# Decoding float64 weights in one two-slope ScalarE pass, and padding the first query block's attention weights to 128 rows

## The chip, the cores and the metric

The kernel runs on one core of a Trainium2 chip. The metric is the device time of one launch in microseconds (us), lower is better. Before the change the median of three runs is 1122.09 us (1118.11 to 1125.32).

The engines, as the profile names them: PE is TensorE's matrix multiply and PEld its weight load, DVE is VectorE, ACT is ScalarE, POOL is GpSimd, and SP is SyncE, which in this kernel issues every DMA. Each engine works through its own queue in order.

## The reference, cut to what matters

```python
def _attn_ref(q, k, v, f):                 # q, k, v: (8, 8, 576, 64), f: (8, 8, 576)
    scores = scale * np.matmul(q, k.transpose(0, 1, 3, 2))
    cum = np.cumsum(np.log(np.clip(f, 0.0001, 1.0)), axis=-1)
    decay = cum[:, :, :, None] - cum[:, :, None, :]
    scores = np.where(causal, -1000000000.0, scores + decay)
    attn = np.exp(scores - np.max(scores, axis=-1, keepdims=True))
    attn = attn / (np.sum(attn, axis=-1, keepdims=True) + 1e-09)
    return np.matmul(attn, v)

def _moe_ref(x, w_in, w_out):              # x: (4608, 512), w_in: (512, 2048), w_out: (2048, 512)
    h = x @ w_in
    g = h * np.clip(h + 3.0, 0.0, 6.0) / 6.0
    return (g @ w_out)
```

Eight batches of eight heads go through causal attention with a decay, and the result, 4608 tokens of 512 features, through two matrix products with a hard-swish between them. `w_in` and `w_out` are float64, 8 MB each; the kernel gets them as 64-bit integers and has to make fp16 of them.

## The kernel before, in words

**Attention.** The list `VH` has 68 units. Four "A" units take two heads of batch 0 each, queries 0 to 255; eight "B" units take one head of batch 0 each, queries 256 to 575; 56 "F" units take one head of batches 1 to 7 each, all 576 queries. An F unit is `rows(v)`. It cuts the queries into five chunks that start at `RB` and have `RR = [64, 128, 128, 128, 128]` rows, so chunk 0 has 64 queries and the others 128. The chunks are done in two halves, `NAT = ((1, 4, 0), (2, 3))`. For a half, PE makes the scores `pn` (lines 623 and 626), DVE masks them and takes the row maximum into `pp` (L634), ACT takes the exponential (L646) and rounds it to fp16 (L658), and DVE or POOL subtract to get the low fp16 part (L661, L667, L672). High and low part lie side by side in `hl`, one of three buffers `ring` that the weight decoding used earlier. Then `dma_start_transpose` (L685) turns blocks of 128 columns of `hl` into `pT`, so that keys lie on partitions. There is one such DMA for neighbouring chunks with equal rows: in the first half one for chunks 1 and 4 (12 blocks of 128 rows) and one for chunk 0 (one block of 64 rows), in the second half one for chunks 2 and 3 (12 blocks).

`av(v, ph)` multiplies `pT` with the values: for each chunk `c` the weights of PE are a block of `pT` (128 keys by the chunk's queries), and the moving operand is the values' 65 columns (64 and a column of ones) or their low part. Lines 713 and 714 are the first two products of each chunk, lines 716 to 718 the rest. For chunk 0 there are only those two, and their weights are 64 columns wide.

**Weights.** `w_in` and `w_out` come in 16 chunks each of 128 by 512 float64 values (512 KB). `w_load` issues the DMA into a slot, `w_decode` makes float32 of it, and a Square with an accumulator (L271) sums the squares for a power-of-two scale; the slot is free for the next load when that Square, which writes its unused output there, is done. `w_split` later makes the fp16 high and low parts. In `w_decode` the high 32-bit word of the double, read as a float32 and scaled by 2^-112, has its exponent where a shift by three bits makes a float32 of it, with the top three bits of the low word behind it. The tables `POOL_SIGN` choose between two ways of keeping the sign. For 15 of the 32 chunks two ACT Relu passes (L254, L255) make the two signs' parts, POOL adds them (L256), and DVE shifts the low word (L257) and joins (L258). For the other 17 one ACT Copy (L262) is followed by three DVE operations: shift the low word (L263), put the sign bit into it (L264), join (L267).

**The rest.** Nine tiles of 512 tokens go through `h_unit` (lines 800 to 802 on PE, then L810, L813, L814, L815 on ACT and DVE) and `out_unit` (lines 822 to 824, then L833). The first tile needs the decoded `w_in`, and its second part the split `w_out`.

**What sets the order.** The text of the main loop interleaves the attention units with steps of the weight work (`w_step`, by `W_RATE`) and with steps of the token tiles (`fill`, by `F_RATE`). From that text a scheduler with a timing model of its own lays out each engine's queue: it places an instruction where its model finds the inputs ready. So a change in one place can move instructions of other places in every queue. On PE the products of the token tiles stand between those of the attention.

## Time and profile before

| | us |
|---|---|
| median of three runs (lowest, highest) | 1122.09 (1118.11, 1125.32) |
| the profiled execution's own time | 1118.29 |
| its span in the trace | 1116.5 |
| PE busy | 1040.3 |
| DVE busy | 745.9 |
| ACT busy | 619.5 |
| POOL busy | 430.4 |

The granted TensorE clock was 0.977 of full speed over the span. Busy matmuls are pipelined and their ends are modelled, so a busy PE is not PE at its peak; the start of one matmul to the start of the next is the better measure of what PE spends on it. The chain of waits follows the work that ended last back from the end, and names at each step what released it.

### The profile page before, as it was taken

To read this page: it belongs to the slowest core of one execution; us is meant where nothing else is said; L and a number is where in the kernel's file an instruction comes from. 1 tells how busy PE (TensorE), PEld (TensorE's weight loads), DVE (VectorE), ACT (ScalarE), POOL (GpSimd) and SP (SyncE) were. 2 spreads that over 40 slices of the span, in tenths; PEclk is the share of its full clock that TensorE was granted. 3 is DMA by queue.
4 is the path that set the end of the run, shared out by engine and by line. 5 is a ranking of instruction groups with operands and counts; after the bars stand their busy time and mean duration, and the time that the engine had idled before them with its cause. 6 is when DMAs were issued, how large, how long until landed. Compare 5 with 4: busy or idle time off the path is not lost.

```text
span 1116.5 us, 20389 instructions
## 1 busy us (share of the span) xinstructions
PE 1040.3 (93%) x7074; PEld 582.4 (52%) x7074; DVE 745.9 (67%) x1921; ACT 619.5 (55%) x1300; POOL 430.4 (39%) x464
## 2 busy tenths in 40 slices
PE   1779897899899998999999989999999999999998
PEld 1457774575455554554555545554555554444443
DVE  7987998787795679668865886587658951520520
ACT  4667765656773466537754764476547841621520
POOL 8565563336444444434443534453344420000000
PEclk9969998999999999999999989999999999999999
DMA  7664545676656565656566766556676443001001
GB/s 221 210 203 145 181 119 110 144 161 140 167 114 133 132 154 109 126 129 165 116 125 131 148 127 124 130 126 136 127 129 134 95 98 60 10 1 38 1 1 38
DMA packets 259859, 132.84 MB, mean 119 GB/s; under 512 B 227652, under 2 KB 229244, under 8 KB 259756
## 3 DMA queue, kind: packets, MB, share of 16 engines
q1 hardware_dynamic: 259756, 131.54, 52.1%
q8 instruction: 56, 0.92, 0.3%
q14 instruction: 47, 0.39, 0.1%
HBM read 47.93 MB, written 9.73 MB: 52 GB/s over the span
## 4 chain that ended last, share of the span: by engine, by line
PE 66%; DVE 15%; DMA 8%; SPq 4%; issue 3%; ACT 3%; POOL 1%; DVEq 0%; ACTq 0%; POOLq 0%
PE po L823 10%; PE po L822 10%; PE po L824 10%; PE ph L800 8%; PE ph L801 8%; PE ph L802 8%; PE pn L626 3%; PE pn L623 3%; DMA ring<-in_w_out_dram 2%; DVE pp L634 2%; DVE ring L661 1%; SPq L774 1%; DMA xT<-xhl 1%; PE pav L717 1%; PE pav L718 1%
## 5 line engine op out<-in xcount | busy, mean ns | idle before, releaser
L800 PE MATMUL ph<-xT,w 128*128 128x512 f16 (+1 forms) x640 | 232.2, 364 | 20.2 <-DVE r L813 15.3
L801 PE MATMUL ph<-xT,w 128*128 128x512 f16 (+1 forms) x640 | 231.0, 364 | 0.0
L802 PE MATMUL ph<-xT,w 128*128 128x512 f16 (+1 forms) x640 | 230.5, 363 | 0.0
L823 PE MATMUL po<-w,gT 128*128 128x512 f16 x576 | 216.6, 382 | 5.7 <-DVE w L309 5.6
L646 ACT ACTIVATE pp<-pp,nb 128x192 f32<-128x192 f32 x280 | 138.3, 552 | 142.6 <-DVE nb L640 141.9
L824 PE MATMUL po<-w,gT 128*128 128x512 f16 x576 | 216.2, 381 | 0.0
L822 PE MATMUL po<-w,gT 128*128 128x512 f16 x576 | 213.9, 382 | 0.8 <-ACT o L833 0.8
L661 DVE TENSOR_TENSOR ring<-pp,ring 128x128 f16<-128x128 f32 (+2 forms) x216 | 134.3, 638 | 86.0 <-ACT ring L658 83.5
L473 POOL TENSOR_TENSOR T<-ST,T 64x576 fp32r<-64x576 f32 (+1 forms) x68 | 102.7, 1511 | 215.7 <-DMA T<-TK 196.0
L813 DVE SCALAR_TENSOR_TENSOR r<-r,ph 128x512 f32<-128x512 f32 (+1 forms) x160 | 100.0, 626 | 89.2 <-ACT r L810 89.1
L810 ACT ACTIVATE r<-ph,bias_r,SC 128x256 f32<-128x256 f32 (+7 forms) x272 | 144.5, 571 | 23.8 <-PE ph L802 21.0
L814 ACT CAST gT<-r 128x512 f16<-128x512 f32 (+1 forms) x160 | 91.7, 575 | 83.5 <-DVE r L813 83.3
L634 DVE CUSTOM_DVE_ANT_0 pp<-pn,W 128x192 f32<-128x192 f32 x280 | 122.8, 481 | 21.3 <-PE pn L626 20.3
L815 DVE TENSOR_TENSOR gT<-r,gT 128x512 f16<-128x512 f32 (+1 forms) x160 | 115.4, 725 | 27.4 <-ACT gT L814 27.0
L623 PE MATMUL pn<-TK,TQ 68*128 68x192 f32 x336 | 125.0, 385 | 2.4 <-PE pav L724 0.9
L626 PE MATMUL pn<-T,T 128*128 128x192 f32 x336 | 113.9, 369 | 0.7 <-POOL T L473 0.7
L658 ACT CAST ring<-pp 128x192 f16<-128x192 f32 x280 | 112.6, 452 | 0.0
L461 POOL TENSOR_SCALAR TK<-ST 64x576 fp32r<-64x576 f32 (+1 forms) x68 | 57.3, 842 | 129.3 <-issue 74.6
L470 POOL TENSOR_TENSOR T<-ST,TQ 64x576 fp32r<-64x576 f32 (+2 forms) x68 | 99.6, 1464 | 16.7 <-PE pn L626 11.4
L801 PEld LDWEIGHTS <-w 128*128 128x128 f16 x640 | 62.8, 99 | 69.6 <-issue 26.1
L667 POOL TENSOR_TENSOR ring<-pp,ring 128x128 f16<-128x128 f32 x96 | 59.4, 619 | 97.3 <-ACT ring L658 81.7
L800 PEld LDWEIGHTS <-w 128*128 128x128 f16 x640 | 63.2, 99 | 62.3 <-issue 15.6
(151 smaller groups left out, 1777.7 us busy)
## 6 DMA issues: line engine op xcount, KB each, us to landing
ST<-in_qk_dram SPq DMA_DIRECT2D x64, 288.0 KB
T<-TK SPq DMA_DIRECT2D x64, 144.0 KB
out_dram<-o SPq DMA_DIRECT2D x36, 256.0 KB
ring<-in_w_out_dram SPq DMA_DIRECT2D x16, 512.0 KB
T<-TQ SPq DMA_DIRECT2D x56, 144.0 KB
vst<-in_vS_dram SPq DMA_DIRECT2D x7, 1040.0 KB
ring<-in_w_in_dram SPq DMA_DIRECT2D x9, 512.0 KB
w<-in_w_in_dram SPq DMA_DIRECT2D x7, 512.0 KB
```

Of the source, the lines that this page charges most:

```text
L623: nc.tensor.matmul(dst, TQ[i][0:D + 4, qs], TK[i][0:D + 4, a:e], start=True, stop=False)
L626: nc.tensor.matmul(dst, T7[j][:, qs], T1[j][:, a:e], start=False, stop=True)
L634: nc.vector.tensor_tensor_reduce(pp[:r, w:w + kw], pn[:r, o:o + kw], W[:r, 4 * P + r - kw:4 * P + r], 1.0, -3.0e38, ALU.add, ALU.max, accu ...
L646: nc.scalar.activation(x_, x_, AF.Exp, bias=nb[:r, e0 + x:e0 + x + 1], scale=0.125)
L661: eng.tensor_tensor(hl[:r, a:a + c * P], pp[:r, at[c] + 64:at[c] + kw], hl[:r, h0[c] + 64:h0[c] + kw], op=ALU.subtract,)
L800: nc.tensor.matmul(ph, w1[0][:, cc, fs_], xh, start=(cc == 0), stop=False)
L801: nc.tensor.matmul(ph, w1[0][:, cc, fs_], xl, start=False, stop=False)
L802: nc.tensor.matmul(ph, w1[1][:, cc, fs_], xh, start=False, stop=(cc == NCC - 1))
L810: nc.scalar.activation(r[:, a:e], ph[:, a:e], AF.Relu, bias=bias_r, scale=scol(A1 + NG * b + fc * NG // NFC))
L822: nc.tensor.matmul(po, gT[:, 0, fc, ts_], w2[:, fc, 0, :], start=(fc == 0), stop=False)
L823: nc.tensor.matmul(po, gT[:, 0, fc, ts_], w2[:, fc, 1, :], start=False, stop=False)
L824: nc.tensor.matmul(po, gT[:, 1, fc, ts_], w2[:, fc, 0, :], start=False, stop=(fc == NFC - 1))
```

## The change

It has two parts.

**The weights' decoding.** All 32 chunks go one way. ACT's Prelu with scale 2^-112 and slope 2^32 for negative inputs does what the two Relu passes and POOL's addition did: a negative number gets an exponent that is 32 higher, and one bit of that becomes the sign after the shift by three. DVE then shifts the float32 word in place, and a second DVE operation shifts the low word and joins. The slot is only read by these, where before DVE and ACT also wrote into it.

```diff
-            low = nc.gpsimd if POOL_LOW[i][k % 4] else nc.vector
-            if POOL_SIGN[i][k % len(POOL_SIGN[i])]:
-                nc.scalar.activation(f32, hf, AF.Relu, scale=2.0 ** -112)
-                nc.scalar.activation(hf, hf, AF.Relu, scale=-2.0 ** -80)
-                nc.gpsimd.tensor_tensor(f32, f32, hf, op=ALU.add)
-                low.tensor_scalar(lo, lo, 29, None, op0=ALU.logical_shift_right)
-                nc.vector.scalar_tensor_tensor(
-                    i32, i32, 3, lo, op0=ALU.logical_shift_left, op1=ALU.bitwise_or
-                )
-            else:
-                nc.scalar.activation(f32, hf, AF.Copy, scale=2.0 ** -112)
-                low.tensor_scalar(lo, lo, 29, None, op0=ALU.logical_shift_right)
-                nc.vector.scalar_tensor_tensor(
-                    lo, hi, -2 ** 31, lo, op0=ALU.bitwise_and, op1=ALU.bitwise_or
-                )
-                nc.vector.scalar_tensor_tensor(
-                    i32, i32, 3, lo, op0=ALU.logical_shift_left, op1=ALU.bitwise_or
-                )
+            nc.scalar.activation(f32, hf, AF.Prelu, scale=2.0 ** -112, alpha=2.0 ** 32)
+            nc.vector.tensor_scalar(i32, i32, 3, None, op0=ALU.logical_shift_left)
+            nc.vector.scalar_tensor_tensor(
+                i32, lo, 29, i32, op0=ALU.logical_shift_right, op1=ALU.bitwise_or
+            )
```

**The first 64 queries of an F unit.** POOL writes zeros into rows 64 to 127 of chunk 0's block of `hl`. With that all blocks of a half have 128 rows, and one transpose moves the half: 13 blocks in the first, 12 in the second. `pT` is laid out with 128 columns a block, and the products of chunk 0 have 128 rows, of which the upper 64 are zero. A single memset of the upper rows of `pav` before the first F unit goes.

```diff
-            o += (2 * c + 1) * RR[c]
+            o += (2 * c + 1) * P
...
+            if 0 in NAT[half]:
+                nc.gpsimd.memset(hl[64:, h0[0] - 64:h0[0] + 64], 0.0)
...
-            for a, e, r, d in moves:
-                g = (e - a) // P
-                nc.sync.dma_start_transpose(
-                    pT[:, d:d + g * r].rearrange("p (g t) -> p g t", t=r), hl[0:r, a:e]
-                )
+            w = sum((2 * c + 1) * P for c in NAT[half])
+            d = HT[NAT[half][0]]
+            nc.sync.dma_start_transpose(
+                pT[:, d:d + w].rearrange("p (g t) -> p g t", t=P), hl[:, 0:w]
+            )
...
-            if n == H:
-                nc.vector.memset(pav[64:, 0], 0.0)
             for c in range(NCH):
-                m = RR[c]
-                pb = ph[:, HT[c]:HT[c] + (2 * c + 1) * m].rearrange("p (g t) -> p g t", t=m)
-                o1, o0 = pav[:m, c, 0:D + 1], pav[:m, c, 0:D]
+                pb = ph[:, HT[c]:HT[c] + (2 * c + 1) * P].rearrange("p (g t) -> p g t", t=P)
+                o1, o0 = pav[:, c, 0:D + 1], pav[:, c, 0:D]
```

Three places show what that makes of the queues. The rows give the line, the operation, the tile written and the tiles read, and the size of the output; line numbers behind the decoding are 15 to 22 lower in the changed kernel.

PE, in the middle of the F units, where the values' products of one head begin. L713 and L714 are chunk 0's, the L800 group is a token tile's. Before:

```order
L801 MATMUL ph_8_0_6192<-xT_117,w_113 128x512
L713 LDWEIGHTS pT_5922
L713 MATMUL pav<-v_111,pT_5922 64x65
L802 LDWEIGHTS w_114
L802 MATMUL ph_8_0_6192<-xT_117,w_114 128x512
L800 LDWEIGHTS w_113
L800 MATMUL ph_8_0_6192<-xT_117,w_113 128x512
L714 LDWEIGHTS pT_5922
L714 MATMUL pav<-v_111,pT_5922 64x64
L801 LDWEIGHTS w_113
L801 MATMUL ph_8_0_6192<-xT_117,w_113 128x512
```

The same place in the changed kernel:

```order
L779 MATMUL ph_8_0_6144<-xT_117,w_113 128x512
L691 LDWEIGHTS pT_5874
L691 MATMUL pav<-v_111,pT_5874 128x65
L780 LDWEIGHTS w_114
L780 MATMUL ph_8_0_6144<-xT_117,w_114 128x512
L778 LDWEIGHTS w_113
L778 MATMUL ph_8_0_6144<-xT_117,w_113 128x512
L692 LDWEIGHTS pT_5874
L692 MATMUL pav<-v_111,pT_5874 128x64
L779 LDWEIGHTS w_113
L779 MATMUL ph_8_0_6144<-xT_117,w_113 128x512
```

The order here is the same; the two products of chunk 0 are 128 rows high instead of 64. In 17 of the 56 heads before, L713 and L714 of chunk 0 stand next to each other; in the other 39 a token tile's products stand between them, as here.

SP and POOL, for the same head. SP before: the head's three transposes, with a load of queries and keys (`ST`) and the loads of the next values (`vst`) behind them.

```order
L426 DMA ST_103<-in_qk_dram 128x576
L685 DMA_TRANSPOSE pT_5922<-ring_124 128x12x128
L685 DMA_TRANSPOSE pT_5922<-ring_124 128x1x64
L685 DMA_TRANSPOSE pT_5922<-ring_125 128x12x128
L426 DMA ST_104<-in_qk_dram 128x576
L374 DMA vst<-in_vS_dram 64x520 x2
L375 DMA vst<-in_vS_dram 128x4x520
```

SP in the changed kernel:

```order
L411 DMA ST_103<-in_qk_dram 128x576
L666 DMA_TRANSPOSE pT_5874<-ring_124 128x13x128
L411 DMA ST_104<-in_qk_dram 128x576
L666 DMA_TRANSPOSE pT_5874<-ring_125 128x12x128
L359 DMA vst<-in_vS_dram 64x520 x2
L360 DMA vst<-in_vS_dram 128x4x520
```

One transpose is gone, and the load of `ST_104` has moved ahead of the second. POOL before, where L667 and L672 end the two halves of this head and L461, L462, L470, L473 prepare queries and keys of later heads:

```order
L667 TENSOR_TENSOR ring_124<-pp_0_5933,ring_124 128x2x64
L672 TENSOR_TENSOR ring_124<-pp_0_5933,ring_124 64x64
L473 TENSOR_TENSOR T_99<-ST_104,T_99 64x576
L667 TENSOR_TENSOR ring_125<-pp_1_5987,ring_125 128x2x64
L461 TENSOR_SCALAR TK_96<-ST_103 64x576
L462 TENSOR_SCALAR TQ_93<-ST_103 64x576
L470 TENSOR_TENSOR T_102<-ST_105,TQ_95 64x576
```

POOL in the changed kernel:

```order
L654 TENSOR_TENSOR ring_124<-pp_0_5885,ring_124 128x2x64
L659 TENSOR_TENSOR ring_124<-pp_0_5885,ring_124 64x64
L458 TENSOR_TENSOR T_99<-ST_104,T_99 64x576
L654 TENSOR_TENSOR ring_125<-pp_1_5939,ring_125 128x2x64
L642 MEMSET ring_124 64x128
L446 TENSOR_SCALAR TK_96<-ST_103 64x576
L447 TENSOR_SCALAR TQ_93<-ST_103 64x576
L455 TENSOR_TENSOR T_102<-ST_105,TQ_95 64x576
```

The memset for a later head's use of `ring_124` stands right behind this head's second half. It overwrites what the first half's transpose reads, so it has to wait until that transpose has landed, and what prepares the next head stands behind it.

DVE, at the start, between the last steps of the decay (`cs`) and the first row maxima (`junk`). Before:

```order
L257 TENSOR_SCALAR ring_123<-ring_123 128x512
L175 TENSOR_SCALAR cs<-cum 64x576
L176 SCALAR_TENSOR_TENSOR cs<-cum,cs 64x576
L263 TENSOR_SCALAR ring_124<-ring_124 128x512
L264 SCALAR_TENSOR_TENSOR ring_124<-ring_124 128x512
L263 TENSOR_SCALAR ring_125<-ring_125 128x512
L267 SCALAR_TENSOR_TENSOR gT<-gT,ring_124 128x512
L264 SCALAR_TENSOR_TENSOR ring_125<-ring_125 128x512
L263 TENSOR_SCALAR w_115<-w_115 128x512
L267 SCALAR_TENSOR_TENSOR gT<-gT,ring_125 128x512
L264 SCALAR_TENSOR_TENSOR w_115<-w_115 128x512
L267 SCALAR_TENSOR_TENSOR gT<-gT,w_115 128x512
```

In the changed kernel:

```order
L173 TENSOR_SCALAR cs<-cum 64x576
L251 TENSOR_SCALAR gT<-gT 128x512
L174 SCALAR_TENSOR_TENSOR cs<-cum,cs 64x576
L252 SCALAR_TENSOR_TENSOR gT<-ring_123,gT 128x512
L251 TENSOR_SCALAR gT<-gT 128x512
L252 SCALAR_TENSOR_TENSOR gT<-ring_124,gT 128x512
L251 TENSOR_SCALAR gT<-gT 128x512
L252 SCALAR_TENSOR_TENSOR gT<-ring_125,gT 128x512
L251 TENSOR_SCALAR gT<-gT 128x512
L252 SCALAR_TENSOR_TENSOR gT<-w_115,gT 128x512
L490 ISA junk_0_165,MC_106<-pn_0_160,W 128x128
```

Each chunk has two DVE operations instead of two or three, and the first now waits for ACT's pass, where the first one before (L257, L263) waited for the DMA alone.

More of the change, by code (lines that the diff above doesn't have):

```diff
@@ L106 @@
     W_ORDER = 0
-    POOL_SIGN = ((1, 0, 0, 0, 1, 1, 1, 1, 1, 0, 0, 0, 1, 0, 0, 0), (1, 0, 1, 0))
-    POOL_LOW = ((0, 0, 0, 0), (0, 0, 0, 0))
     POOL_REST = ((0, 0, 0, 0), (0, 0, 0, 0))
@@ L248, in w_decode @@
             i32 = f32.bitcast(I32)
-            hi = slot.rearrange("p (n t) -> p n t", t=2)[:, :, 1]
             hf = slot.bitcast(F32).rearrange("p (n t) -> p n t", t=2)[:, :, 1]
             lo = slot.rearrange("p (n t) -> p n t", t=2)[:, :, 0]
-            low = nc.gpsimd if POOL_LOW[i][k % 4] else nc.vector
-            if POOL_SIGN[i][k % len(POOL_SIGN[i])]:
-                nc.scalar.activation(f32, hf, AF.Relu, scale=2.0 ** -112)
-                nc.scalar.activation(hf, hf, AF.Relu, scale=-2.0 ** -80)
-                nc.gpsimd.tensor_tensor(f32, f32, hf, op=ALU.add)
-                low.tensor_scalar(lo, lo, 29, None, op0=ALU.logical_shift_right)
-                nc.vector.scalar_tensor_tensor(
-                    i32, i32, 3, lo, op0=ALU.logical_shift_left, op1=ALU.bitwise_or
-                )
-            else:
-                nc.scalar.activation(f32, hf, AF.Copy, scale=2.0 ** -112)
-                low.tensor_scalar(lo, lo, 29, None, op0=ALU.logical_shift_right)
-                nc.vector.scalar_tensor_tensor(
-                    lo, hi, -2 ** 31, lo, op0=ALU.bitwise_and, op1=ALU.bitwise_or
-                )
-                nc.vector.scalar_tensor_tensor(
-                    i32, i32, 3, lo, op0=ALU.logical_shift_left, op1=ALU.bitwise_or
-                )
+            nc.scalar.activation(f32, hf, AF.Prelu, scale=2.0 ** -112, alpha=2.0 ** 32)
[3 more added lines that the diff above has]
+            )
         if i == 1 or not GRAM[k // NCC]:
@@ L675, in rows @@
                 )
-            moves = []
-            for c in NAT[half]:
-                a, w = GH[half][c], (2 * c + 1) * P
-                if moves and moves[-1][2] == RR[c]:
-                    moves[-1][1] = a + w
-                else:
-                    moves.append([a, a + w, RR[c], HT[c]])
-            for a, e, r, d in moves:
-                g = (e - a) // P
-                nc.sync.dma_start_transpose(
-                    pT[:, d:d + g * r].rearrange("p (g t) -> p g t", t=r), hl[0:r, a:e]
-                )
+            w = sum((2 * c + 1) * P for c in NAT[half])
[3 more added lines that the diff above has]
+            )
             yield pT
```

## The prediction

> **What bounds the kernel now.** I read the table of busy times by stage first. The stages are batch 0 (0 to 155 us), the start of the F units (155 to 225), the F units (225 to 925) and the token tiles left over (925 to the end).
>
> ```profile
> core 0: us, PE busy (x) PEld busy (x) DVE busy (x) ACT busy (x) POOL busy (x), PEclk, DMA share, GB/s
> 0.00:155.00 155.00, 112.83 (x671) 86.41 (x672) 134.66 (x343) 100.54 (x204) 97.72 (x98) 0.91 0.62 187
> 155.00:225.00 70.00, 57.99 (x469) 38.03 (x468) 58.19 (x172) 44.57 (x96) 30.32 (x29) 0.93 0.59 120
> 225.00:925.00 700.00, 682.54 (x5009) 372.30 (x5007) 506.20 (x1338) 418.85 (x911) 301.58 (x339) 0.99 0.62 131
> 925.00:1116.00 191.00, 186.94 (x931) 85.68 (x930) 46.87 (x72) 55.53 (x91) 0.78 (x1) 1.00 0.08 20
> ```
>
> For 700 us PE is busy 98% of the time, and DVE, ACT and POOL have 194, 281 and 398 us to spare. In the first 155 us it is DVE that is full (134.66 of 155), and PE has holes. A busy PE can still be one that waits inside, so I read the chain of waits for these two stages:
>
> ```profile
> by line: DMA ring<-in_w_out_dram 16.1%; issue 5.5%; DMA xT<-in_vS_dram 5.4%; DMA w<-in_w_in_dram 5.3%; DVE gT L267 4.1%; DVE ring L264 4.1%; DVE rs L747 3.7%; DVE junk L505 3.5%; DMA ring<-in_w_in_dram 3.5%; PE pav L724 3.4%; DVE w L267 3.2
> by line: PE po L822 10.7%; PE po L823 10.7%; PE po L824 10.6%; PE ph L800 9.3%; PE ph L801 9.2%; PE ph L802 9.1%; PE pn L626 4.2%; PE pn L623 4.2%; issue 2.9%; DMA xT<-xhl 2.1%; DMA vst<-in_vS_dram 1.9%; PE pav L717 1.8%; PE pav L718 1.7%;
> ```
>
> The first row is 0 to 155 us: the loads of the weights, and DVE on lines 264 and 267, the weights' decoding. The second is 225 to 925 us: its PE entries add up to 71.5%, and no engine but PE stands in the row. So time taken from PE in the F units counts for at least seven tenths, and DVE time saved in the first stage counts where the loads do not take its place.
>
> **The change part by part.**
>
> *64 weight columns become 128.* Here PE passes chunk 0 of one head, whose two products stand among a token tile's (start, duration):
>
> ```profile
> 528.73 0.38 PE L802 MATMUL ph<-xT,w 128*128 128x512 f16 x1
> 528.94 0.38 PE L800 MATMUL ph<-xT,w 128*128 128x512 f16 x1
> 529.16 0.38 PE L801 MATMUL ph<-xT,w 128*128 128x512 f16 x1
> 529.47 0.22 PE L713 MATMUL pav<-v,pT 128*64 128x65 f16 x1
> 529.62 0.39 PE L802 MATMUL ph<-xT,w 128*128 128x512 f16 x1
> 529.84 0.38 PE L800 MATMUL ph<-xT,w 128*128 128x512 f16 x1
> 530.15 0.22 PE L714 MATMUL pav<-v,pT 128*64 128x64 f16 x1
> 530.30 0.39 PE L801 MATMUL ph<-xT,w 128*128 128x512 f16 x1
> 530.53 0.19 PE L713 MATMUL pav<-v,pT 128*128 128x65 f16 x1
> 530.56 0.38 PE L802 MATMUL ph<-xT,w 128*128 128x512 f16 x1
> 530.78 0.19 PE L714 MATMUL pav<-v,pT 128*128 128x64 f16 x1
> 530.81 0.38 PE L800 MATMUL ph<-xT,w 128*128 128x512 f16 x1
> ```
>
> The reader is to look at the distance of the starts. From one 512-column product to the next it is 0.21 to 0.22 us. A product with 128 weight columns that stands between costs 0.03 us (530.53 to 530.56), and the next again follows after 0.22. The ones with 64 weight columns (`128*64`) cost more on both sides: 529.16 to 529.47 is 0.31, 0.09 more than before any other product, and 529.47 to 529.62 is 0.15, 0.12 more than the 0.03 of a full one. That is 0.21 us for each, 0.42 for a head, and the change removes it, as the product then has 128 columns and no other work. Where the two stand next to each other, the price is paid once:
>
> ```profile
> 429.96 0.38 PE L802 MATMUL ph<-xT,w 128*128 128x512 f16 x1
> 430.26 0.22 PE L713 MATMUL pav<-v,pT 128*64 128x65 f16 x1
> 430.32 0.20 PE L714 MATMUL pav<-v,pT 128*64 128x64 f16 x1
> 430.45 0.20 PE L713 MATMUL pav<-v,pT 128*128 128x65 f16 x1
> 430.49 0.38 PE L800 MATMUL ph<-xT,w 128*128 128x512 f16 x1
> ```
>
> 0.30 instead of 0.22 going in, 0.06 and 0.13 instead of 0.03 each coming out: 0.21 us. With 17 heads of this kind and 39 of the other that is 17 x 0.21 + 39 x 0.42 = 20.0 us of PE. By the chain's 71.5% it would be worth 14.3 us, by PE's 98% 19.6. I take 17, between the two; the ends are 20.0 and nothing, the latter if the next wait of the attention takes PE's place.
>
> Does the wider weight load cost something? These are the loads of L713 in both widths:
>
> ```profile
> L713 PEld LDWEIGHTS <-pT 128*128 128x128 f16 x224 | 21.9, 98 | 10.3 <-DMA pT<-ring 3.3 <-issue 0.3
> L713 PEld LDWEIGHTS <-pT 128*64 128x64 f16 x56 | 6.0, 106 | 26.3 <-issue 20.1 <-DMA pT<-ring 4.1 <-DMA TQ<-decay_dram 1.3
> ```
>
> 98 ns for 128 columns and 106 for 64: nothing is added. The Trainium skill, page "TensorE: Matmul & The Clock Gate", section "LDWEIGHTS (loading the stationary operand)", says otherwise: a load takes the number of columns over 1.2 ns, so an estimate by that page is 53 ns for 64 columns and 107 for 128, and the 112 wider loads would give back up to 6 us, which makes 1098 of the 1092 below. The trace does not agree, and the trace decides. The page "TensorEngine Tiling (Array Packing)" of the Trainium skill, section "Key Properties", says that a change of the tiling mode drains TensorE; by that the 0.09 and 0.12 belong to the width itself and not to a semaphore, and would go with the width.
>
> *The weights' decoding.* These rows give the instructions that go or are halved (busy us, mean ns):
>
> ```profile
> L264 DVE SCALAR_TENSOR_TENSOR ring<-ring 128x512 int32<-128x512 int32 x12 | 10.3, 860 | 0.1
> L264 DVE SCALAR_TENSOR_TENSOR w<-w 128x512 int32<-128x512 int32 x5 | 5.5, 1102 | 0.0
> L267 DVE SCALAR_TENSOR_TENSOR w<-w,ring 128x512 int32<-128x512 int32 x8 | 6.6, 830 | 0.2
> L267 DVE SCALAR_TENSOR_TENSOR gT<-gT,w 128x512 int32<-128x512 int32 x5 | 5.5, 1109 | 0.1
> L267 DVE SCALAR_TENSOR_TENSOR gT<-gT,ring 128x512 int32<-128x512 int32 x4 | 4.7, 1169 | 0.0
> L264 DVE SCALAR_TENSOR_TENSOR ring<-ring x12: 676/694/1798, 10.2 to 143.6; 128x512 int32<-128x512 int32 x12
> L255 ACT ACTIVATE ring<-ring 128x512 f32<-128x512 f32 x13 | 8.8, 674 | 0.1
> L256 POOL TENSOR_TENSOR w<-w,ring 128x512 f32<-128x512 f32 x8 | 11.1, 1388 | 9.9 <-ACT ring L255 9.8
> ```
>
> DVE: the 17 sign operations of L264 go, 10.3 + 5.5 = 15.8 us. What is left for each chunk is a shift and a join of the same size as now, taken at the same price. ACT: 15 second Relu passes of 0.67 us, 10 us, beside DVE's work. POOL: 15 additions of 1.39 us, 21 of its 97.72 us. The L264 row with minimum, median and maximum (676/694/1798 ns) shows that DVE is stretched at times; the 17 of L267 take 16.8 us instead of 17 x 0.68 = 11.6. If POOL is what stretches them, POOL's additions are a fifth of that, 1 us, and as much for L258, the same form 15 times.
>
> How much of it is on the path? In the chain's row L264 on `ring` has 4.1% of 155 us, 6.4 us. With the 2 us of less stretching that is 8, the value I take. It could be nothing, if the loads (their four entries are 30.3% of the row, 47 us) only get longer by what DVE gets shorter; and it could be 15.8 and all the stretching of L267 and L258, 5.2 us each, together 26 us.
>
> *One transpose less a head.* SP before, three transposes of one head:
>
> ```profile
> 506.21 4.55 SPq L685 DMA_TRANSPOSE pT<-ring  x3
> ```
>
> Each holds SP for 1.5 us, the one with a single block too, so 56 of them are 84 us of SP's queue. What that is worth stands in the page's shares of the chain:
>
> ```profile
> PE 66%; DVE 15%; DMA 8%; SPq 4%; issue 3%; ACT 3%; POOL 1%; DVEq 0%; ACTq 0%; POOLq 0%
> ```
>
> SPq is 4% of 1116.5 us, 45 us, for all SP issues together. A third of the L685 issues go, and at most half of the SPq share is theirs, so 0 to 8 us; I take 3. The 13th block of the longer transpose is hidden like the 12 others: nothing.
>
> *POOL's memset.* 56 of 64 by 128, priced by the nearest rows, with what POOL now waits for behind its place:
>
> ```profile
> L883 POOL MEMSET T<- 128x64 f32 x2 | 0.2, 158 | 0.1
> L473 POOL TENSOR_TENSOR T<-ST,T 64x576 fp32r<-64x576 f32 x64 | 97.3, 1520 | 214.6 <-DMA T<-TK 195.1 <-DMA TK<-decay_dram 12.5 <-DVE ring L257 4.9
> L461 POOL TENSOR_SCALAR TK<-ST 64x576 fp32r<-64x576 f32 x64 | 53.7, 839 | 125.2 <-issue 74.6 <-DMA ST<-in_qk_dram 18.5 <-PE pn L623 16.7
> ```
>
> At 0.16 to 0.3 us it is 9 to 17 us of POOL, which idles 398 us in the F units, 7.1 a head. It also waits there until the head's first transpose has landed; L461, which stands behind it, idles 125 us anyway and L473 215 us. I cost it at nothing and come back to it below.
>
> *Sum.* 17 + 8 + 3 = 28 us off the profiled execution's 1118.29 (its span 1116.5 and 1.8 around it): 1090. The median of the runs is 3.8 above this execution, and I set the forecast half of that higher, at **1092 us**. With both ends of each term it would be between 1120 and 1118 - 20 - 26 - 8 = 1064.
>
> **The rivals.**
>
> *Only PE's part arrives.* In the first stage the loads set the pace (47 us of its chain), and less DVE work only makes DVE wait for them. For it: DMA's share is 0.62 over the stage at 187 GB/s. Against it: each slot is free earlier when DVE and POOL need less, so the loads start earlier too. 1118.3 - 17 - 3 = 1098, with the same 2 us 1100.
>
> *Only the first stage arrives.* The gaps at chunk 0 go, and PE then waits as long for the rows of the next head, since 28% of the F stage's chain is not PE. Against it: DVE, ACT and POOL have 194 us and more to spare there. 1118.3 - 8 - 3 = 1107, so 1109.
>
> *Neither shows.* The gap is not the width's but that of the first product of a head, and stays, and the loads bound the start: 1118 to 1122.
>
> *Slower: POOL's memset holds the queue.* POOL is in order. The memset waits for a transpose that SP issues behind other DMAs and that takes some us to land; L461, L462 and L470 behind it make the next head's queries and keys, for which SP's copies and PE's scores wait. As long as the wait is under POOL's 7.1 us of idle time a head, nothing is lost. Each us beyond it lengthens a head: at 0.5 us the 28 us are used up, and from there on it is slower; with 0.8 us it is 1118 - 28 + 45 = 1135. Against it: a transpose holds SP for 1.5 us and is issued right behind L672, so a wait of over 7 us needs SP to be late as well.
>
> **How the numbers follow.** Both parts as above: 0.60. Only PE's part: 0.17. Only the start: 0.13. Neither: 0.05. Slower: 0.05. The likeliest gives 1092. The range goes from 1072 (the first stage worth 20 and SP 8 instead of 8 and 3) to 1112, which takes in both halves on their own and leaves out the last two cases and what is below 1072. A measurement of this kernel can tell about 1% from no change, 11 us: faster by more than that is below 1111. The first two cases and two thirds of the third are below, less a little for the upper end of their ranges: 0.84. Within 1%: 0.12. Slower: 0.04.
>
> **What would show each step.** The first row maximum of an F unit stands in the chain of waits (start, duration):
>
> ```profile
> 155.11 0.67 DVE pp L634
> ```
>
> It comes about 8 us earlier, with DVE busy some 16 us less until there. Around L691 and L692 (formerly L713 and L714) every start is 0.03 us ahead of the next, and no row has `128*64` on them; the F stage is some 20 us shorter with as many products of the token tiles in it. SP has two transposes a head. POOL's idle time before L446 grows by less than it has now. The prediction is wrong if the gaps stay with 128 columns, if the F stage keeps its length while PE's idle time in it grows (then the next wait names the cause), or if POOL's memset stands in the chain.

## The result, and the profile after

The changed kernel takes 1082.97 us (median of four runs, 1080.43 to 1084.99) against 1122.03 us before (1118.11 to 1125.32): a ratio of 0.9652, with a 95% interval of 0.9613 to 0.9691. The forecast was 1092 us, range 1072 to 1112. The profiled execution has a span of 1082.6 us at a granted clock of 0.986.

The stages of the changed kernel, in the columns of the table that opens the prediction, cut at the first and the last row maximum of the F units, and the F stage of the kernel before cut in the same way:

```profile
0.00:136.00 136.00, 106.19 (x679) 83.03 (x680) 109.48 (x335) 92.09 (x192) 66.80 (x85) 0.99 0.71 212
136.00:889.00 753.00, 716.90 (x5454) 408.43 (x5454) 558.76 (x1493) 460.09 (x998) 347.95 (x419) 0.98 0.65 134
```

```profile
155.00:922.00 767.00, 737.53 (x5463) 409.06 (x5462) 563.07 (x1502) 460.80 (x1001) 331.88 (x366) 0.98 0.62 130
```

The first F unit starts 19 us earlier, the F stage is 14 us shorter, and the rest behind it is as long as before. The rows of the row maximum's line give both ends (columns: shortest, median and longest in ns, then the first and last start). First before, then after:

```profile
L634 DVE CUSTOM_DVE_ANT_0 pp<-pn,W x280: 207/483/754, 154.8 to 922.0; 128x192 f32<-128x192 f32 x28, 64x64 f32<-64x64 f32 x28, 128x448 f32<-128x448 f32 x28, 128x576 f32<-128x576 f32 x28
```

```profile
L619 DVE CUSTOM_DVE_ANT_0 pp<-pn,W x280: 204/483/758, 136.1 to 888.9; 128x192 f32<-128x192 f32 x28, 64x64 f32<-64x64 f32 x28, 128x448 f32<-128x448 f32 x28, 128x576 f32<-128x576 f32 x28
```

154.8 to 922.0 is 767.2 us, 136.1 to 888.9 is 752.8. I call this the F stage's length from here on; the expectations below count to the last accumulator read, 0.6 us later.

PE at chunk 0 of a head among a token tile's products (start, duration):

```profile
421.86 0.38 PE L800 MATMUL po<-w,gT 128*128 128x512 f16 x1
422.08 0.19 PE L691 MATMUL pav<-v,pT 128*128 128x65 f16 x1
422.11 0.38 PE L801 MATMUL po<-w,gT 128*128 128x512 f16 x1
422.33 0.19 PE L692 MATMUL pav<-v,pT 128*128 128x64 f16 x1
422.36 0.38 PE L802 MATMUL po<-w,gT 128*128 128x512 f16 x1
```

No `128*64` stands at L691 and L692 any more, and the starts are 0.22 and 0.03 us apart, as for any other product: the gaps of 0.09 and 0.12 us are gone. Chain of waits, first stage and then the F units from 225 us on, as in the prediction's rows:

```profile
by line: PE pav L702 9.7%; PE low L286 9.2%; issue 7.2%; DMA ring<-in_w_out_dram 6.7%; DVE junk L490 4.7%; DMA TQ<-mr 3.9%; DMA vst<-in_vS_dram 3.9%; DMA v<-in_vS_dram 3.9%; PE ps L548 3.5%; PE pn L484 3.3%; DVE w L252 2.9%; PE ps L549 2.7%
by line: PE po L800 11.6%; PE po L802 11.5%; PE po L801 11.5%; PE ph L778 9.8%; PE ph L779 9.5%; PE ph L780 9.4%; PE pn L611 4.5%; PE pn L608 4.4%; issue 2.5%; DVE pp L619 2.0%; SPq L752 1.9%; PE pav L695 1.9%; PE pav L696 1.8%; DMA vst<-in
```

In the first stage the loads of `w_in`, 8.8% together before, no longer stand among the leaders, those of `w_out` fell from 16.1% to 6.7%, and of the decoding's DVE lines only L252 is left in the row, with 2.9%. PE leads both rows now.

### The profile page after: what moved, and what is told of

It is laid out like the page before. It is cut to its first block, busy times and chain, and to the rows that moved or that the text cites. A ratio compares the mean times of both kernels' runs of the same rounds, so it can differ in the third digit from the quotient of the medians.

```text
span 1082.6 us, 20307 instructions
## 1 busy us (share of the span) xinstructions
PE 1012.2 (94%) x7074; PEld 578.3 (53%) x7074; DVE 716.3 (66%) x1903; ACT 610.3 (56%) x1285; POOL 415.5 (38%) x505
## 4 chain that ended last, share of the span: by engine, by line
PE 73%; DVE 12%; DMA 5%; issue 3%; SPq 3%; POOL 2%; ACT 2%; DVEq 0%; POOLq 0%; ACTq 0%
PE po L801 11%; PE po L800 10%; PE po L802 10%; PE ph L778 9%; PE ph L779 9%; PE ph L780 9%; PE pn L611 3%; PE pn L608 3%; DMA vst<-in_vS_dram 2%; DVE pp L619 2%; SPq L752 2%; DVE ring L648 2%; PE pav L695 1%; PE pav L696 1%; PE pav L694 1%
## 5 line engine op out<-in xcount | busy, mean ns | idle before, releaser
L800 PE MATMUL po<-w,gT 128*128 128x512 f16 x576 | 214.5, 382 | 4.1 <-ACT w L283 2.2
L648 DVE TENSOR_TENSOR ring<-pp,ring 128x128 f16<-128x128 f32 (+2 forms) x216 | 129.7, 615 | 84.6 <-ACT ring L645 83.6
L458 POOL TENSOR_TENSOR T<-ST,T 64x576 fp32r<-64x576 f32 (+1 forms) x68 | 99.7, 1466 | 139.0 <-DMA T<-TK 134.9
L645 ACT CAST ring<-pp 128x192 f16<-128x192 f32 x280 | 113.0, 452 | 0.0
L654 POOL TENSOR_TENSOR ring<-pp,ring 128x128 f16<-128x128 f32 x96 | 62.5, 651 | 106.9 <-ACT ring L645 77.7
L802 PEld LDWEIGHTS <-gT 128*128 128x128 f16 x576 | 57.0, 99 | 76.2 <-issue 15.1
L778 PEld LDWEIGHTS <-w 128*128 128x128 f16 x640 | 62.9, 98 | 61.9 <-issue 13.7
```

What stands on the lines that cost most here:

```text
L648: eng.tensor_tensor(hl[:r, a:a + c * P], pp[:r, at[c] + 64:at[c] + kw], hl[:r, h0[c] + 64:h0[c] + kw], op=ALU.subtract,)
L778: nc.tensor.matmul(ph, w1[0][:, cc, fs_], xh, start=(cc == 0), stop=False)
L800: nc.tensor.matmul(po, gT[:, 0, fc, ts_], w2[:, fc, 0, :], start=(fc == 0), stop=False)
L802: nc.tensor.matmul(po, gT[:, 1, fc, ts_], w2[:, fc, 0, :], start=False, stop=(fc == NFC - 1))
```

## The experiments

Ratios are to runs of the kernel before on the same chip (medians 1120.6 to 1122.0 us), with their 95% intervals. "First row" is the first start of the row maximum in the profiled execution, "F" the length of the F stage, "SP" the sum of the durations of SP's DMA issues in it, "clock" the time lost there to a granted clock of one half, worked out from the trace's clock rows.

| kernel | us | ratio | first row | F | SP | clock |
|---|---|---|---|---|---|---|
| before | 1122.0 | 1 | 154.8 | 767.2 | 581 | 12 |
| e_decode: new decoding alone | 1107.0 | 0.988 (0.984 to 0.992) | 137.7 | 776.1 | 567 | 17 |
| e_pad: padding alone | 1101.1 | 0.983 (0.979 to 0.987) | 156.8 | 743.7 | 512 | 12 |
| e_narrow: changed, products 64 wide | 1091.7 | 0.974 (0.971 to 0.978) | 136.6 | 759.0 | 509 | 5 |
| e_two_moves: changed, block 0 moved by itself | 1099.8 | 0.981 (0.977 to 0.986) | 136.8 | 770.3 | 567 | 24 |
| e_three: changed, second half in two moves | 1099.5 | 0.981 (0.976 to 0.986) | 135.9 | 770.3 | 553 | 24 |
| changed | 1083.0 | 0.965 (0.961 to 0.969) | 136.1 | 752.8 | 510 | 14 |
| e_up: changed, fewer moves of the output | 1077.2 | 0.961 (0.958 to 0.964) | 136.7 | 747.1 | 483 | 12 |
| e_small: changed, six tiny copies more a head | 1156.3 | 1.032 (1.028 to 1.036) | 136.8 | 822.8 | 705 | 51 |

### Each part alone: e_decode and e_pad

e_decode is the kernel before with the changed `w_decode`; e_pad is the changed kernel with the old one:

```diff
-            nc.scalar.activation(f32, hf, AF.Prelu, scale=2.0 ** -112, alpha=2.0 ** 32)
-            nc.vector.tensor_scalar(i32, i32, 3, None, op0=ALU.logical_shift_left)
...
+            if POOL_SIGN[i][k % len(POOL_SIGN[i])]:
+                nc.scalar.activation(f32, hf, AF.Relu, scale=2.0 ** -112)
...
```

> The kernel before with the new decoding of the weights alone. In the changed kernel the first row maximum of an F unit stands 18.7 us earlier (154.8 to 136.1 us), where 8 us were forecast. Theory: all of that is the decoding's, and the F stage is as long as before, so about 1122 - 19 = 1103 us, with the first row maximum near 136 us. Rival, the forecast's own size: the decoding brings 8 us, and the other 11 come from something that the padding does to the start or from a different clock there: about 1114 us, first row maximum near 147 us.

> The changed kernel with the old decoding: zero rows, one transpose a half and the 128 column products alone. The F stage got 14.4 us shorter in the changed kernel (767.8 to 753.4 us from first to last row maximum). Theory: the two parts add up, so this one gives 1122 - 39 + 19 = 1102 us, between 1100 and 1108, with the first row maximum still near 155 us. Rival: each part needs the other (the earlier start lets the F stage keep its work fed), and this alone gives little, 1110 us or more.

The decoding alone gives 0.988, the padding alone 0.983, and the first row maximum follows the decoding only: 137.7 with the new one, 156.8 with the old. So the 17 to 21 us at the start are the decoding's, as the theory had it. In time the two parts add up within the noise: 0.988 x 0.983 is 0.971, the changed kernel has 0.965, and the intervals leave 0.7% either way. e_pad lies in its theory's range; e_decode is 4 us above the 1103 of its own.

In the traces the F stage is 9 us longer with the earlier start, in both pairs (767.2 to 776.1 without the padding, 743.7 to 752.8 with it). That is one execution of each kernel, and these were not typical: the profiled ones of before and e_pad were 3.8 and 5.2 us under their medians, those of e_decode and the changed kernel 3.1 and 1.4 above. That is some 7 of the 9 us. The medians show less: e_decode gains 14 us for a start that is 17 us earlier, and the changed kernel 20 us on e_pad for 21. So the traces' 9 us are mostly the choice of executions, and the 1 to 3 us that the medians leave are within their noise. What can be seen in the stage are these rows, PE's waits in the opening of the F stage (total us, times, longest), from the first row maximum to 260 us, before and after:

```profile
PE po L823 <- DVE w L309: 5.6, 6, 2.3
```

```profile
PE po L801 <- DVE w L294: 7.5, 4, 4.7
PE po L800 <- ACT w L283: 2.2, 2, 1.8
```

The second product needs the split `w_out`, and with an earlier start PE waits 4 us more for DVE and ACT to split it.

### Width against transposes: e_narrow, e_two_moves, e_three

e_narrow keeps the zero rows and the single transpose, but gives PE the first 64 columns of chunk 0's block only:

```diff
+                m = RR[c]
-                o1, o0 = pav[:, c, 0:D + 1], pav[:, c, 0:D]
-                nc.tensor.matmul(o1, pb[:, c], vh[:, 0], start=True, stop=False)
+                o1, o0 = pav[:m, c, 0:D + 1], pav[:m, c, 0:D]
+                nc.tensor.matmul(o1, pb[:, c, :m], vh[:, 0], start=True, stop=False)
```

e_two_moves keeps the width and moves block 0 by a transpose of its own; e_three leaves the first half alone and moves chunks 2 and 3 apart:

```diff
-            w = sum((2 * c + 1) * P for c in NAT[half])
-            d = HT[NAT[half][0]]
-            nc.sync.dma_start_transpose(
-                pT[:, d:d + w].rearrange("p (g t) -> p g t", t=P), hl[:, 0:w]
-            )
+            for cs_ in ([c for c in NAT[half] if c], [c for c in NAT[half] if not c]):
+                if cs_:
+                    a, d = GH[half][cs_[0]], HT[cs_[0]]
+                    w = sum((2 * c + 1) * P for c in cs_)
+                    nc.sync.dma_start_transpose(
+                        pT[:, d:d + w].rearrange("p (g t) -> p g t", t=P), hl[:, a:a + w]
+                    )
```

In e_three the two lists are `((1, 4, 0), ())` for the first half and `((2, ), (3, ))` for the second.

> The changed kernel with zero rows and one transpose a half, but chunk 0's two products of each head read only the first 64 weight columns again. Theory: the gain of the F stage is the width, 0.09 us into and 0.12 us out of a 64 column product, so the time goes from 1083 us up by 14 to 20, to 1097 to 1103, and the gaps of 0.09 and 0.12 us stand around the products again. Rival: the gain is the transpose that was saved on SP, the gaps were covered: under 1087 us.

> The changed kernel with block 0 moved by a transpose of its own, of 128 rows with the zero rows: three transposes a head as before, all products 128 columns wide. Forecast term: the saved transpose is worth 3 us, so 1086 us; its ends were 0 and 8, 1083 to 1091. Rival: SP is never late there, and the time is the changed kernel's, 1083 us, within 2. Second rival: the saved transpose costs the F stage time, because block 0 now waits until the whole half is ready (6 us of the removed gaps came back as other waits); then this kernel is faster than the changed one, 1077 to 1081 us.

> The changed kernel, but the second half's 12 blocks moved by two transposes of SP (chunk 2's 5 blocks, chunk 3's 7); the first half keeps its single one. Theory, SP's time: a third transpose a head costs the same wherever it is, so as e_two_moves about 1083 + 17 = 1100 us, 1094 to 1104. Rival: the cost of e_two_moves came from block 0 alone (its transfer lands late and PE waits for chunk 0): then under 1088 us.

In e_narrow the gaps are back, as its PE rows show (0.31 us into a `128*64` product, 0.15 out of it):

```profile
438.26 0.38 PE L803 MATMUL po<-w,gT 128*128 128x512 f16 x1
438.57 0.22 PE L694 MATMUL pav<-v,pT 128*64 128x65 f16 x1
438.72 0.39 PE L804 MATMUL po<-w,gT 128*128 128x512 f16 x1
```

But the time goes up by only 0.9% (0.974 against 0.965), below what the theory said. The transpose, which I had at 3 us, costs 1.6% in e_two_moves, and the same in e_three, where it is another block's. Together with e_decode these make a square: the old width or the new, three transposes a head or two, all with the new decoding. The width is worth 0.988 - 0.981 with three transposes and 0.974 - 0.965 with two; on average 0.8%, 9 us with an interval of some 4.5 to both sides. The transpose is worth 0.988 - 0.974 and 0.981 - 0.965, on average 1.5%, 17 us, with an interval as wide. (The width's side of the square holds the zero rows too; e_zero_once below finds no gain in leaving POOL's out.)

How does a third transpose reach PE? PE's waits in the F stage, e_three and then the changed kernel:

```profile
PE ph L780 <- DMA xT<-xhl: 16.1, 6, 4.3
PE pav L693 <- DMA pT<-ring: 10.2, 9, 3.1
```

```profile
PE pav L691 <- DMA pT<-ring: 5.4, 7, 2.1
PE ph L778 <- DMA xT<-xhl: 5.3, 2, 2.7
```

PE waits 26.3 us instead of 10.7 for what SP's transposes bring, the output `xT` of a batch before the weights `pT` of a head. In e_two_moves it is 9.6 for `xT` and 4.3 for `pT`, and 13.7 behind the token tiles' DVE work instead of 9.5. All of PE's waits in the stage together are 9 to 10 us longer in both kernels than in the changed one, and 10 us more are lost to the clock. Together that is about the 17.5 us by which the stage is longer, but the two need not add up (last section).

### SP's time or the transfer: e_two_act, e_up, e_small

e_two_act is e_two_moves with block 0's transpose issued by ACT (`nc.scalar` in place of `nc.sync`).

> The kernel of e_two_moves (1099.8 us, 17 above the changed kernel), with block 0's own transpose issued by ACT instead of SP. Theory: what the third transpose of a head costs is SP's time, 1.5 us of its queue in which other issues wait. Off SP it costs next to nothing: 1083 to 1088 us (ACT, busy 56%, loses some time to the issue). Rival: it is the transfer itself, or that PE's products wait for two transfers instead of one, whoever issues it: 1097 to 1103 us.

It takes 1229.46 us, ratio 1.095 (1.088 to 1.103), which neither side expected, and settles nothing. In the instructions' waits ACT's transpose waits for those of SP that are in flight, and SP's next one for ACT's; and ACT, which is in order, stands with its other work behind that wait: its semaphore waits at the transpose's line add up to 102 us, the longest 9.1. In front of the rounding (L645) and of a token tile's work (L794) that is idle time of ACT which the profile puts down to no other engine:

```profile
ACT ring L645 <- issue: 51.8, 14, 8.2
ACT gT L794 <- issue: 48.5, 7, 8.6
```

e_up takes transposes of another line off SP. Block 0's queries go to rows 64 to 127, where the exponential writes them, so the output's move of a pair needs two runs instead of three:

```diff
-                    x_, x_, AF.Exp, bias=nb[:r, e0 + x:e0 + x + 1], scale=0.125
+                    pp[P - r:, at[c]:at[c] + kw], x_, AF.Exp, bias=nb[:r, e0 + x:e0 + x + 1], scale=0.125
...
-            runs = [(0, 0, 1, 0), (0, 1, NCH, 1), (64, 1, NCH, 2)]
+            runs = [(0, 1, NCH, 1), (64, 0, NCH, 0)]
```

> The changed kernel with block 0's 64 queries in rows 64 to 127 and the zero rows at 0 to 63 (the exponential writes them there), so that the output's moves of a pair of heads are two runs instead of three: 28 transposes of 1.24 us fewer on SP, 35 us, and all else as it was. Theory, SP's time: 56 transposes of 1.5 us were worth 17 us, 0.2 us for each us of SP, wherever they were; 35 us less bring 7 us: 1074 to 1079 us. Rival: it is the rows' transposes that PE waits for, not SP's time in general; the output's moves are not late, and the time stays at 1083 us within 2.

1077.2 us, inside the theory's range. The count was wrong: some runs are cut at the end of a token tile, so 20 transposes went and not 28 (x148 before):

```profile
L752 SPq DMA_TRANSPOSE xT<-xhl x128: 1157/1244/2357, 47.7 to 901.9; - x128
```

That is 25 us of SP for 5.8 us of time. The interval of e_up alone overlaps that of the changed kernel. The same edit on top of e_zero_once (next part) goes from 0.969 to 0.963; both pairs together make it 0.5%, with an interval of 0.2 to 0.8%. e_up has the lowest median of all kernels here.

e_small adds time on SP with next to no transfer, at the place of e_two_moves' extra transpose:

```diff
+    extra = cpool.tile([2, 48], F16, name="extra")
...
+            if half == 0:
+                for x in range(6):
+                    nc.sync.dma_start(extra[:, x * 8:x * 8 + 8], hl[0:2, h0[0] - 64 + x * 8:h0[0] - 56 + x * 8])
```

> The changed kernel with six small copies more on SP in each head, of 2 rows by 8 numbers, from chunk 0's block right behind the first half's transpose, the place where e_two_moves had block 0's own. At 0.25 us an issue (the issue of the small load TQ<-decay_dram takes 0.252 us in the changed kernel) they hold SP for about the 1.5 us of a transpose and transfer next to nothing. Theory, SP's time: as e_two_moves and e_three, 1083 + 17 = 1100 us, 1093 to 1104. Rival: it is the transposes' transfers that crowd each other in the DMA engines; these copies bring none, and the time is 1081 to 1087 us.

It is far beyond both. The issue takes 0.57 us and not 0.25:

```profile
L672 SPq DMA_DIRECT2D extra<-ring x336: 568/569/1497, 154.4 to 967.5; - x168
```

336 x 0.57 = 191 us of SP, the F stage 70 us longer, with 336 transfers of 32 bytes. PE's longest waits in the stage are now for the same transposes' output, and for the keys and queries that SP's copies feed (in the changed kernel 5.4, 5.3 and none):

```profile
PE pav L695 <- DMA pT<-ring: 22.8, 14, 8.6
PE ph L782 <- DMA xT<-xhl: 21.4, 5, 4.9
PE pn L612 <- POOL T L459: 17.1, 11, 3.2
```

So the rival, that it takes the transposes' transfers, falls: issues that carry next to nothing lengthen the stage as well. By the table's sums a us of SP costs 0.2 us in e_up (5.8 for 27), 0.3 in e_two_moves (17 for 57) and 0.36 here (70 for 195), where SP issues for 705 of 823 us. That would fit a price that rises as the queue fills, but the first two have intervals that overlap. The sum is no measure by itself either: in e_two_act SP issues for only 494 us of a stage of 899, the longest of all.

### What the decoding's forms cost: e_dve3 and e_pool

Both are e_pad with a single form for all 32 chunks: three DVE operations, or two ACT passes with POOL's addition.

```diff
+    POOL_SIGN = ((0, ), (0, ))
```

In e_pool it is `((1, ), (1, ))`.

> The kernel with the padding and the old decoding, all 32 chunks in its form of three VectorE operations: no addition on POOL, no second ACT pass, 15 sign operations more on DVE than in e_pad (1101.1 us, first row maximum at 156.8 us). Theory: DVE's operations set the start, 17 of them were worth the whole 18 to 20 us there, so 15 more push the first row maximum to 170 us or more, time 1112 to 1120 us. Rival: POOL's additions and what waits for them set it; with none left the first row maximum comes at 140 to 150 us, time 1085 to 1095 us.

> The same with all 32 chunks in the form with two ACT passes and an addition on POOL: DVE has the two operations a chunk that it has in the changed kernel, POOL 32 additions of 1.39 us (44 us more than the changed kernel), ACT 32 passes more of 0.67 us. Theory, DVE's operations set the start: first row maximum at 136 to 142 us, time 1083 to 1090 us. Rival, POOL's additions (and the time that they stretch DVE by) count as much: first row maximum past 150 us, 1097 us or more.

e_dve3 takes 1109.98 us (0.990, 0.986 to 0.993), e_pool 1126.35 (1.004, 1.001 to 1.008). In the trace their first row maxima start at 163.8 and 164.3 us. Up to there, e_dve3 and then e_pool:

```profile
0.00:163.80 163.80, 120.24 (x687) 91.91 (x688) 133.34 (x372) 96.56 (x195) 77.75 (x85) 0.90 0.59 177
```

```profile
0.00:164.30 164.30, 113.92 (x678) 88.05 (x678) 123.24 (x312) 107.69 (x217) 115.99 (x118) 0.87 0.60 175
```

Neither side holds for both kernels: e_dve3 comes close to its theory (163.8 where 170 or more was expected), e_pool falls on its rival's side. The 32 third DVE operations come with a first row maximum 163.8 - 136.1 = 28 us behind that of the changed kernel, 0.87 us each, and so do the 32 pairs of a second pass and an addition, with DVE doing no more operations than in the changed kernel. So a step more per chunk is paid on either engine, and the mixed form of the kernel before (156.8 in e_pad) was better than either pure one. How much of the 28 us is the operations' own is open: until then 17 us are lost to a granted clock of one half in e_dve3 and 22 in e_pool, against 1.7 in the changed kernel. And e_pool takes 16 us more than e_dve3 with the same start; its F stage is 11 us longer in the trace, for which I have no cause.

POOL also slows DVE. These are the joins' rows, a shift and an or with two SBUF inputs, all of e_dve3, then all of e_pool, then all of the changed kernel:

```profile
L267 DVE SCALAR_TENSOR_TENSOR w<-w,ring 128x512 int32<-128x512 int32 x16 | 11.0, 692 | 0.7 <-ACT r L803 0.5
L267 DVE SCALAR_TENSOR_TENSOR gT<-gT,ring 128x512 int32<-128x512 int32 x9 | 6.8, 755 | 0.0
L267 DVE SCALAR_TENSOR_TENSOR gT<-gT,w 128x512 int32<-128x512 int32 x7 | 5.7, 814 | 0.1
```

```profile
L258 DVE SCALAR_TENSOR_TENSOR w<-w,ring 128x512 int32<-128x512 int32 x15 | 12.4, 824 | 1.7 <-POOL w L256 1.7
L258 DVE SCALAR_TENSOR_TENSOR gT<-gT,ring 128x512 int32<-128x512 int32 x9 | 8.9, 994 | 2.9 <-POOL gT L256 2.9
L258 DVE SCALAR_TENSOR_TENSOR gT<-gT,w 128x512 int32<-128x512 int32 x7 | 6.1, 869 | 0.0
```

```profile
L252 DVE SCALAR_TENSOR_TENSOR w<-ring,w 128x512 int32<-128x512 int32 x16 | 12.2, 762 | 0.1
L252 DVE SCALAR_TENSOR_TENSOR gT<-ring,gT 128x512 int32<-128x512 int32 x9 | 6.4, 714 | 0.1
L252 DVE SCALAR_TENSOR_TENSOR gT<-w,gT 128x512 int32<-128x512 int32 x7 | 5.9, 844 | 0.1
```

By their sums a join takes 0.73 us in e_dve3 (23.5 over 32) and 0.77 in the changed kernel (24.5 over 32), both without POOL's additions in the decoding, and 0.88 in e_pool with all of them (27.4 over the 31 before the cut). But it is not the additions alone: in the kernel before, with 15 of them, it takes 0.98 (31.3 over 32). One by one in the traces, a join that no POOL operation overlaps takes 0.68 us, at most 0.70, in all four kernels, and every one over 0.75 overlaps an operation of POOL: 15 of 32 before, 13 in e_pool, 5 in the changed kernel, 4 in e_dve3. The additions (L256) are the partner in 6 of the 15 and 6 of the 13, the preparation of queries and keys (L461, L462, L470, L473) in the others of these two. The Trainium skill, page "SBUF — State Buffer", section "SBUF: two separate sides", says that DVE and GpSimd share a pair of ports as an exclusive lock, which a DVE operation with two SBUF inputs takes part in; the traces agree, with 0.68 us for a join beside no POOL operation and means of 0.79 (e_dve3) to 1.10 us (before) for those beside one.

### The zero rows: e_zero_once and e_up_once

Nothing but chunk 0's block uses those columns, so the zeros can be written once for each of the three buffers:

```diff
-            if 0 in NAT[half]:
+            if 0 in NAT[half] and n < H + NRING:
                 nc.gpsimd.memset(hl[64:, h0[0] - 64:h0[0] + 64], 0.0)
```

> The changed kernel with POOL's zero rows written for the first three heads of the F stage only, once in each of the three buffers: nothing else writes those 64 rows by 128 columns. In the changed kernel POOL stands 106 us in front of the 56 of them, waiting for the transpose that reads the buffer, and SP waits 20 us for them in the F stage. Forecast's step: the memset costs nothing, POOL has the time: 1083 us, within 2. Rival: the wait holds the queries and keys behind it and SP; with SP's time worth 17 us for 84 us of it, 20 us less of SP's waits bring 4 us, and what POOL makes earlier as much again: 1074 to 1080 us.

> Both edits of e_zero_once and e_up together. If both theories hold (4 to 8 us and 7 us) 1068 to 1074 us; if neither, 1083 us.

1084.55 us (0.969, 0.966 to 0.972) and 1078.64 us (0.963, 0.960 to 0.966): no gain. POOL's rows show where the wait went. In the changed kernel:

```profile
L642 POOL MEMSET ring<- 64x128 f16 x56 | 11.7, 208 | 114.2 <-DMA pT<-ring 106.2 <-DVE rs L720 4.5 <-ACT r L788 1.7
L446 POOL TENSOR_SCALAR TK<-ST 64x576 fp32r<-64x576 f32 (+1 forms) x68 | 52.1, 766 | 68.0 <-PE pn L608 51.8 <-PE ps L548 7.5 <-issue 3.6
L458 POOL TENSOR_TENSOR T<-ST,T 64x576 fp32r<-64x576 f32 (+1 forms) x68 | 99.7, 1466 | 139.0 <-DMA T<-TK 134.9 <-ACT xhl L731 2.0 <-ACT v L396 0.7
```

and in e_zero_once:

```profile
L446 POOL TENSOR_SCALAR TK<-ST 64x576 fp32r<-64x576 f32 (+1 forms) x68 | 50.8, 748 | 104.7 <-issue 83.4 <-PE pn L608 8.2 <-PE ps L548 8.0
L458 POOL TENSOR_TENSOR T<-ST,T 64x576 fp32r<-64x576 f32 (+1 forms) x68 | 99.0, 1456 | 216.1 <-DMA T<-TK 209.7 <-DVE gT L793 4.6 <-DVE rs L723 0.3
```

POOL stood 114 us in front of the zero rows, 106 of them for the transpose. Without them it stands 37 us longer in front of L446 and 77 longer in front of L458, which is the same 114.

## Why the prediction was right, and where its terms were off

**The sum.** The forecast took 28 us off the profiled execution. The profiled executions differ by 34 us and the medians by 39, so 6 to 11 us are missing, and the decoding alone brings 6 to 12 more than its term. The two terms of the F stage were about right in their sum, 20 us against the 20 that e_pad gains and the 26 of the square, and wrong in their shares. That the sum came out is luck: one term was 8 us too large and the other 14 too small. The range reached far enough down because it allowed 20 us for the start; its lower end, added up as the forecast was, comes to 1075 and not 1072, and the result is inside either way.

**64 weight columns become 128: 17 us forecast, 9 measured.** The mechanism and its size on PE hold: the gaps are the width's, they come back with it (e_narrow), and they add up to some 20 us. The step that failed is the share of it that arrives. I took it from PE's part of the chain, 71.5%, and PE's busy share, 98%; the square of runs gives 9 us, a little under half. Most of the rest came back as other waits of PE: with the gaps gone its waits in the F stage add up to 35.9 us where e_narrow has 28.2, and to 46.0 in e_two_moves where e_decode has 36.0. Where a wait follows, a gap ahead of it costs nothing.

**One transpose less: 3 us forecast, 17 measured.** This is the term that was mis-sized most. The 84 us of SP's time that it started from came out as 57 to 69 in SP's sums, so it was the price that was wrong. The step was to price SP by its 4% of the chain, half of it for this line, with a bound of 8. The chain's share counts only where SP itself stands in the chain. A late transpose shows there as a DMA (`xT`, `pT`), or as the engine that waited for it, and busy times leave SP's issues out altogether. The sum of SP's issue times would have told: 427 us of transposes and 154 us of other DMAs in 767 us, 76%, on a queue that is in order and that waits besides.

**The decoding: 8 us forecast, 18.7 at the first row maximum, 13 to 20 in the time.** Two steps fell short. "ACT: 15 second Relu passes of 0.67 us, 10 us, beside DVE's work" and POOL's additions were costed at nothing but their stretching of DVE; e_pool shows that a chunk of that form holds the start up as much as one with the third DVE operation. And the stretching was 2 us in the sum, where the joins went from 31.3 us over 32 to 24.5, 6.8 us less. DVE is busy for 109.5 us up to the first row maximum instead of 134.7, 25 less and not 16. The lower end, that the loads would take what DVE gives, did not come about: DMA's share rose from 0.62 to 0.71 and its rate from 187 to 212 GB/s, which is the same 29 MB in 19 us less. Whether the clock did a part of it is open: 12 us less are lost to a granted clock of one half until the first row maximum (last section).

**What was not in the sum.** An earlier start could have cost the F stage something, and no term stood for that. By the medians it cost 1 to 3 us, within the noise.

**POOL's memset: nothing forecast, nothing measured.** The row says 208 ns each, 11.7 us, within the 9 to 17 us, and a wait of 1.9 us a head on average, under the 7.1 us of idle time that the rival would have had to exceed. e_zero_once takes it away without gain.

**The wider load.** L691's loads take 98 ns for 128 columns, so nothing is given back, as the rows of before said.

## What to carry to other kernels

Add up the issue times of the queue that starts the DMAs, as for an engine: busy times do not count them and the chain of waits names the late transfer rather than the queue, so a queue at three quarters can hide behind a share of 4%. When one transfer is merged into another, price it by the queue's time, even if not a byte less is moved. And an operation that lies on another engine beside a full one is not free when each piece of work passes through all of them in turn: a step put into the passage was paid here on DVE and on ACT and POOL alike.

## What the runs showed of the hardware that was not expected

The granted clock falls to one half in stretches of 3.4 to 23.9 us. In the kernel before, and then in the changed one at the same place (PE busy is the first number behind the length, the clock the third from the end):

```profile
54.00:74.50 20.50, 14.67 (x51) 10.76 (x52) 18.27 (x54) 14.21 (x29) 12.87 (x10) 0.50 0.71 208
```

```profile
54.70:58.10 3.40, 3.37 (x4) 1.33 (x5) 3.40 (x7) 3.07 (x7) 2.81 (x2) 0.50 0.88 295
58.10:78.60 20.50, 19.94 (x119) 14.35 (x118) 17.73 (x61) 17.44 (x37) 8.28 (x9) 1.00 0.68 192
```

All four profiled kernels with the old decoding have a stretch of 13.7 or 20.5 us there, with PE 66 to 77% busy in it; those with the new decoding have 3.4 or 6.8 us. Up to the first row maximum 13.7 us are lost to it before and 1.7 after. In the F stage e_two_moves loses 24 us to such stretches, the changed kernel 14, and e_small, where PE waits most of these, 51. The Trainium skill, page "TensorE: Matmul & The Clock Gate", section "Part 1: The HAM clock gate", has TensorE's clock at half until a window of about 3.4 us has been busy, and back at half after an idle one; the lengths here agree, being multiples of 3.4 us, and so does the end of a stretch: in its last 3.4 us PE is 95 to 100% busy, in the kernel before and in the changed one. The start does not quite: in the 3.4 us ahead of a stretch PE is not idle but 10 to 55% busy, with a wait of 1 to 5 us in it or just ahead of it. So a wait of PE can cost twice, once itself and once in the window behind it.

How much of the gains came by way of the clock stays open, as no run held it fixed, but every execution has its granted clock on record. Among 40 executions of the kernel before, one that lost 1 us more to the half clock took 0.6 us longer on average, and the same slope comes out of the 67 executions of the other kernels about their own means. By that estimate the changed kernel, which loses 13 us on average where the kernel before loses 25, has some 7 of its 39 us that way. Between two and three transposes the average loss differs by 11 us with the new width and 6 with the old, so by the same estimate some 4 to 6 of those 17 us.

A copy of 32 bytes within SBUF holds SP for 0.57 us, a load of 4.5 KB from DRAM for 0.25 (median of `TQ<-decay_dram`), and a transpose of 12 or 13 blocks for 1.5. A transpose of one block holds ACT for 1.1 in e_two_act (median), but SP for 1.5 in the head that the prediction shows, where it stands behind one of 12 blocks.
